# The start of a fused dynamic convolution and feed-forward kernel: first softmax part in two pieces, mask built first, first weights in two loads, row picks between the first units

## The chip, the cores and the metric

The kernel runs on one core of one Trainium2 chip. The time is device microseconds of one execution. The core has a matrix engine (TensorE, PE in the profile; PEld is its weight load), VectorE (DVE), ScalarE (ACT), GpSimd (POOL) and SyncE (SP, which only issues transfers here). They run side by side and wait for one another through semaphores.

## The reference, cut to what matters

Each token has, for each of 8 heads, 7 weights. They go through a softmax and weigh the token's own row of x and the six before it, head by head. The result feeds a feed-forward layer with a squared relu.

```python
w = weight_gen - np.max(weight_gen, axis=-1, keepdims=True)      # (8, 4096, 8, 7)
w = np.exp(w); w = w / (np.sum(w, axis=-1, keepdims=True) + 1e-09)
x_unf = x_pad[:, idx, :].reshape(B, S, K, H, group)              # K = 7, H = 8, group = 24
y = np.einsum('bshk,bskhg->bshg', w, x_unf).reshape(B * S, 192)
h = np.maximum(y @ w_in, 0.0)                                    # w_in: 192 x 2048
out = h * h @ w_out                                              # w_out: 2048 x 192
```

## The kernel before

Tokens are worked in blocks: blocks 0 and 1 of 512 tokens, all later ones of 1024. A block's work is: softmax weights (ScalarE exp, VectorE sum, reciprocal and scale into a tile `v`), rows of `v` brought into the order of the tokens (`wr`), products of `wr` with a band mask that give a banded matrix (`bd`), a convolution as matmuls of x with `bd` into PSUM (`yp`), a cast to fp16 (`y`), and then feed-forward units. A unit is 4 matmuls with w_in in blocks 0 and 1 (6 later) into a PSUM tile `h`, a relu on ScalarE (`t`), and for two units together a squaring on VectorE (`g`). The second matrix product with w_out (`o`) follows in pieces.

For the first two blocks there is no time to send the rows through memory. A "row pick" takes them out of `v` with matmuls against a 0/1 matrix `sel`, eight for one tile of 128 tokens, and ScalarE copies the result out of PSUM. Block 0 and block 1 need five picks each, all from the first softmax part `s0` (8 rows a partition, and 6 rows of the part that follows).

```python
def scale(self, lo, hi, eng):                     # v = ex * rcp, four instructions per 8 rows
    while lo < hi:
        n = min(SL - lo % SL, hi - lo)
        for g in range(HP):
            eng.tensor_tensor(out=..., in0=self.ex[:, lo : lo + n, g],
                in1=self.rcp[:, lo : lo + n, g].unsqueeze(2).broadcast_to((P, n, KK, 2)), op=AluOp.mult)
        lo += n
# [...]
def select_rows(j, s, tiles, places):             # one row pick per tile of 128 tokens
    for i, (pool, tag) in zip(tiles, places):
        pr = pool.tile([P, H * SL], f32, name="pr", tag=tag)
        for r in range(s.r):                      # s.r = 8; HALO = 6
            nc.tensor.matmul(out=pr, lhsT=sel[:, c : c + P], rhs=s.v[:, HALO + r]..., start=(r == 0), stop=(r == s.r - 1))

def copy_rows(j, tiles):                          # PSUM -> wr on ScalarE
    nc.scalar.copy(out=wr_t[j][:, i]..., in_=pr_t.pop((j, i)))

def st_band(j, tiles):                            # bd = wr * mask on VectorE
    nc.vector.tensor_tensor(out=bd_t[j]..., in0=wr_t[j]..., in1=mask..., op=AluOp.mult)
# [...]
spin(21)                                          # 21 warm-up matmuls of 512 columns
row_select(); band_mask()                         # sel, then mask, on GpSimd
s0.load(nc.sync); x_load_f32(0)
load_w_in(w_st, 0, nc.sync)                       # first half of w_in, fp32
load_w_in(w_i[:, 1, 0], 1, nc.gpsimd)             # second half, cast in the transfer
x_load(1); s1.load(nc.gpsimd)
s0.exp(0, s0.rh); s0.total(0, s0.rh); s0.recip(0, s0.rh); s0.scale(0, s0.rh, nc.vector)
# [... row picks, copies and bands of block 0, x casts ...]
st_conv_first(0, next_rows)                       # convolution of block 0; after its first two
                                                  # tiles a row pick of block 1 each, after the
                                                  # second the cast of w_st (ScalarE and VectorE)
select_rows(1, s0, ROW_ORDER[2:4], (o1, o0)); copy_rows(1, ROW_ORDER[2:4])
# [... w_out loads ...]
plans = {
    0: "u P B1 u u u E1 C S1 u u M u u",          # u unit, P row pick, B bands, E exp, C convolution,
    1: "L3 u u B2 M E2 B3 u M E2 u u S2 S2 u M u C u M",   # S rest of softmax, M piece of the second product
    2: "L4 u u u E3 M u u u M B4 u u u u M B5 S3 u u u u M u C E3 u",
    3: "L5 L6 u u u M S3 u u u M u M E4 u u B6 u M u M B7 u u u E4 M u M C S4 u",
}
```

The plan strings give the order in which the steps are written; each engine works through its own instructions in that order.

Of the kernel before, what the change touches and what calls it, by code (L numbers as in the profile page):

```python
# [9 lines left out]
def kernel(  # L10
# [26 lines left out]
    nc = tc.nc  # L37
    f32 = mybir.dt.float32
    f16 = mybir.dt.float16

    B, S, D = x.shape
# [9 lines left out]
    P = 128  # L51
# [16 lines left out]
    BASE = -24  # L68
    starts = [BASE + STEP * i for i in range(NT)]
    bounds = [0, 104, 208, 312, 416, TB]  # L70
    ROW_ORDER = (0, 1, 2, 3, 4)

    AluOp = mybir.AluOpType
    AxisX = mybir.AxisListType.X
# [20 lines left out]
    w_i = const.tile([P, WQ, 2, NQ + NQ // 2], f16, name="w_i")  # L95
    w_p = const.tile([P, WQ, 2, NQ + NQ // 2], f16, name="w_p")
    w_o = const.tile([P, NF, Dm], f16, name="w_o")
    mask = const.tile([P, P, 2], f16, name="mask")
    FIRST = 8
    NSEL = TB + TB - P + FIRST - 1 + P  # L100
# [13 lines left out]

    def band_mask():

        nc.gpsimd.memset(mask, 1.0)
        for sign, base in ((1, 0), (-1, KK - 1)):
            nc.gpsimd.affine_select(
                out=mask, in_=mask, pattern=[[sign, P], [0, 2]], compare_op=AluOp.is_ge,  # L120
                fill=0.0, base=base, channel_multiplier=-sign,
            )

    x_st = {}

    def load_w_in(dst, q, eng):  # L130
        c = q * NQ
        eng.dma_start(out=dst[:, 0:NQ], in_=moe_w_in[0:P, c : c + NQ])
        for r0 in (0, RT):
            eng.dma_start(
                out=dst[r0 : r0 + RT, NQ:], in_=moe_w_in[P:D, c : c + NQ // 2]
            )
            c += NQ // 2

    def cross_w_in(q):
        for r0, r1 in ((0, RT), (RT, 0)):  # L140
# [182 lines left out]
    def x_load(j):  # L323
        x_t[j] = p_x.tile([P, NT, D], f16, name="xt")
        block_load(j, x_t[j], x[j // NBB], D, nc.gpsimd)
# [7 lines left out]
    def x_cast(j, copy, lo, hi):  # L333
        if j not in x_t:
            x_t[j] = p_x.tile([P, NT, D], f16, name="xt")
        copy(
            out=x_t[j][:, lo:hi].rearrange("p t d -> p (t d)"),
            in_=x_st[j][:, lo * D : hi * D],
        )
# [23 lines left out]
    def select_rows(j, s, tiles, places):  # L363

        if j not in wr_t:
            wr_t[j] = p_wr.tile([P, NT, HP, SL * 2], f16, name="wr")
        for i, (pool, tag) in zip(tiles, places):
            pr = pool.tile([P, H * SL], f32, name="pr", tag=tag)
            a = max(j % NBB * TB + tile_start(j, i), 0) - s.t0
            for r in range(s.r):  # L370
                c = a + FIRST - 1 - r
                nc.tensor.matmul(  # L372
                    out=pr, lhsT=sel[:, c : c + P],
                    rhs=s.v[:, HALO + r].rearrange("p g c e -> p (g c e)"),
                    start=(r == 0), stop=(r == s.r - 1),
                )
            pr_t[(j, i)] = pr
# [54 lines left out]
                        for q in (2 * k, 2 * k + 1):  # L432
                            yield later, s, i, q, half, a, b, base

    def st_conv_first(j, between=None):

        s = BLOCKS[j][0]
        y = p_y.tile([P, NK, TB], f16, name="y")
        y_t[j] = y
        if j == 0:  # L440
            yps = [ps_h.tile([P, TB], f32, name="yp", tag="h") for _ in range(2)]
        else:
            yp = ps_h.tile([P, 2, TB], f32, name="yp", tag="h")
            yps = [yp[:, k] for k in (0, 1)]
        places = [(q, 32 * q, 0) for q in range(4)]
        places += [(q, r0 + 32 * (q - 4), 1) for r0 in (0, RT) for q in (4, 5)]
        for i in ROW_ORDER:
            lo, b = bounds[i], bounds[i + 1]
            hi = lo + (STEP if tile_start(s, i) == starts[i] else b - lo)
            bd = bd_t[s][:, H * lo : H * hi].rearrange("p (g c e) -> p g e c", g=HP, e=2)  # L450
            for later in (True, False):
                for q, p0, k in places:
                    _, ha, hb, pre = quads[q]
                    m, h = (32, hb) if later else (pre, ha)
                    nc.tensor.matmul(  # L455
                        out=yps[k][p0 : p0 + m, lo:b],
                        lhsT=x_t[s][:, i, 32 * q : 32 * q + m],
                        rhs=bd[:, h // 2, h % 2, 0 : b - lo],
                        start=True,
                        stop=True,  # L460
                        skip_group_check=True,
                        tile_position=(0, p0),
                    )
            if between:
                between(i)
        if j == 0:
            nc.scalar.copy(out=y[:, 0], in_=yps[0])
            nc.vector.tensor_copy(out=y[:, 1], in_=yps[1])
        else:
            nc.scalar.copy(out=y[:, 0:2], in_=yp)  # L470
# [186 lines left out]
    with nc.allow_low_precision("fp16 matmul pipeline"), tc.manual_schedule():  # L657
# [22 lines left out]
        for v in v_first:  # L680
            nc.vector.memset(v, 0.0)

        wp = ps_o.tile([P, TB], f32, name="wp", tag="o0")

        def spin(n):
            for i in range(n):
                nc.tensor.matmul(out=wp, lhsT=warm[:, 0:P], rhs=warm, start=True, stop=True)

        s0, s1, s2 = parts[:3]
        spin(21)  # L690
        row_select()
        band_mask()
        s0.load(nc.sync)
        w_st = p_wg.tile([P, (R + HALO) * HK], f32, name="w_st", tag="wg")[:, 0 : NQ + NQ // 2]
        x_load_f32(0)
        load_w_in(w_st, 0, nc.sync)
        load_w_in(w_i[:, 1, 0], 1, nc.gpsimd)
        x_load(1)
        s1.load(nc.gpsimd)
        s0.exp(0, s0.rh)  # L700
        s0.total(0, s0.rh)
        s0.recip(0, s0.rh)
        s0.scale(0, s0.rh, nc.vector)
        x_cast(0, nc.scalar.copy, 0, 1)
        x_cast(0, nc.scalar.copy, 1, 3)
        o0, o1, ring = (ps_o, "o0"), (ps_o, "o1"), (ps_h, "h")
        select_rows(0, s0, ROW_ORDER, (o1, ring, ring, ring, o0))
        copy_rows(0, ROW_ORDER[:2])
        x_cast(0, nc.scalar.copy, 3, NT)
        copy_rows(0, ROW_ORDER[2:])  # L710
        for i in ROW_ORDER:
            st_band(0, (i,))

        def next_rows(i):
            n = ROW_ORDER.index(i)
            if n < 2:
                select_rows(1, s0, (i,), ((o1, ring)[n],))
                copy_rows(1, (i,))
            if n == 1:
                c = (NQ + NQ // 2) // 2  # L720
                nc.scalar.copy(out=w_i[:, 0, 0, 0:c], in_=w_st[:, 0:c])
                nc.vector.tensor_copy(out=w_i[:, 0, 0, c:], in_=w_st[:, c:])

        st_conv_first(0, next_rows)
        select_rows(1, s0, ROW_ORDER[2:4], (o1, o0))
        copy_rows(1, ROW_ORDER[2:4])

        nc.gpsimd.tensor_copy(out=gate, in_=w_st[:, 0:1])
        for q in range(4):
            load_w_out(q, 4)  # L730
        s2.load(nc.gpsimd)
        x_load(2)
        nc.gpsimd.memset(v_big, 0.0)

        steady = "MuMuuu" * 3 + "MuuuMCu"
        steady_spread = "MuMuuu" * 2 + "MuCMuuu" + "MuMuuu"
        plans = {  # L740
# [4 lines left out]
        }  # L745


# [110 lines left out]
        for j in range(NBLK):  # L858
            if j + 2 < NBLK:
                load_rows(j + 2)  # L860
            if j == 1:
                for q in range(WQ):
                    cross_w_in(q)
            u = 0
            for step in plans[j].split():
                kind, n = step[0], int(step[1:] or 0)
                if kind == "u":
                    st_unit(j, u)
                    u += 1
                elif kind == "M":  # L870
                    next(mm2)
                elif kind == "C" and j + 1 < NBLK:
                    st_conv(j + 1)
                    if j == 0:
                        x_load(3)
                    elif j + 2 < NBLK:
                        for k in range(BLOCKS[j + 2][0], sum(BLOCKS[j + 2])):
                            x_load(k)
                    if j == 5:
                        load_w_spread()  # L880
                    elif j == 6:
                        cross_w_spread()
                elif kind == "E":
                    parts[n].exp(*next(parts[n].exps))
                elif kind == "S":
                    soft(parts[n])
                elif kind == "B":
                    st_bands(n)
                elif kind == "P":
                    select_rows(1, s0, ROW_ORDER[4:], (o1,))  # L890
                    copy_rows(1, ROW_ORDER[4:])
                elif kind == "L":
                    parts[n].load(nc.sync)

# [46 lines left out]
```

The softmax here doesn't subtract the row's maximum and nothing guards it: scores larger than these inputs give would overflow.

## Time and profile before

| | before |
|---|---|
| time, median of 3 (lowest to highest) | 731.81 us (731.55 to 732.17) |
| span of the profiled execution | 730.0 us |
| PE / DVE / ACT / POOL busy | 724.1 / 626.8 / 612.2 / 99.8 us |
| first unit of block 0 starts | 12.71 us |
| second convolution starts | 16.33 us |
| granted PE clock | 1.00 in all stretches asked for |

The busy times are sums over the whole span. The chain of work that ended last is followed back from the last instruction, step by step, to what released it. In a row of the timeline the bracket at the end gives how long the engine stood idle before it and for whom. The lines themselves stand with the prediction.

### The profile page before, as it was taken

What the parts mean: (1) busy time and instruction counts of PE and PEld (TensorE: products, weight loads), DVE (VectorE), ACT (ScalarE), POOL (GpSimd) and SP (SyncE); (2) the same over time, 40 slices, a digit from 0 to 9 for tenths busy, and PEclk for the clock granted to TensorE, in tenths of its full rate; (3) what the DMA queues carried; (4) which work ended last, traced back from release to release, by engine and by line L of the source; (5) the groups of instructions that cost most, each with busy time, mean ns of one, the idle gap of its engine ahead of it and who ended that gap; (6) DMA issues with size and microseconds to landing.
All of it is one profiled execution on the core that took longest, in us unless ns stands there. A gap on an engine that the chain in (4) does not pass through costs nothing.

```text
span 730.0 us, 30988 instructions
## 1 busy us (share of the span) xinstructions
PE 724.1 (99%) x14053; PEld 528.0 (72%) x14053; DVE 626.8 (86%) x836; ACT 612.2 (84%) x733; POOL 99.8 (14%) x145
## 2 busy tenths in 40 slices
PE   8999999999999999999999999999999999999998
PEld 4657788777777777777777777777777777777777
DVE  7998998998898988888988888988889988778753
ACT  5999888888888888888888888888888888888883
POOL 8131223321001100011001010010000110001000
PEclk9999999999999999999999999999999999999999
DMA  9555455685345452455432554343544325444012
GB/s 202 118 105 115 82 96 105 132 149 129 86 66 138 90 92 59 82 117 124 76 64 61 136 104 88 56 77 116 107 84 86 57 52 119 66 87 78 30 45 68
DMA packets 125984, 68.30 MB, mean 94 GB/s; under 512 B 85321, under 2 KB 122140, under 8 KB 125340
## 3 DMA queue, kind: packets, MB, share of 16 engines
q0 software_dynamic: 46192, 19.43, 22.9%
q1 hardware_dynamic: 79516, 46.79, 22.4%
q8 instruction: 110, 1.80, 1.1%
q14 instruction: 22, 0.18, 0.1%
q10 hardware_dynamic: 144, 0.10, 0.0%
HBM read 50.18 MB, written 28.70 MB: 108 GB/s over the span
## 4 chain that ended last, share of the span: by engine, by line
PE 98%; ACT 1%; DVE 0%; DMA 0%; issue 0%
PE o L621 47%; PE h L572 44%; PE yp L493 4%; PE h L557 2%; PE yp L527 1%; DMA wg<-in_weight_gen_dram 0%; PE yp L455 0%; ACT y L538 0%; DVE v_first L260 0%; PE pr L372 0%; ACT t L586 0%; DVE ssum L245 0%; ACT ex L238 0%; DVE rcp L252 0%; ACT wr L381 0%
## 5 line engine op out<-in xcount | busy, mean ns | idle before, releaser
L586 ACT ACTIVATE t<-h 128x1024 f16<-128x1024 f32 x512 | 496.4, 1026 | 60.3 <-PE h L572 58.8
L621 PEld LDWEIGHTS <-g 64*128 64x128 f16 (+1 forms) x8032 | 344.3, 94 | 55.0 <-issue 2.2
L621 PE MATMUL o<-w_o,g 64*128 64x192 f16 (+1 forms) x8032 | 380.1, 243 | 0.1
L590 DVE TENSOR_TENSOR g<-t 128x2048 f16<-128x2048 f16 (+1 forms) x287 | 307.4, 1105 | 30.1 <-ACT t L586 29.9
L572 PE MATMUL h<-y,w_p 64*128 64x512 f16 x2400 | 291.7, 376 | 0.0
L572 PEld LDWEIGHTS <-w_p 64*128 64x128 f16 x2400 | 113.9, 94 | 94.7
L395 DVE TENSOR_TENSOR bd<-wr,mask 128x4160 f16<-128x4160 f16 (+4 forms) x90 | 149.6, 1686 | 1.3 <-ACT wr L381 0.7
L637 DVE TENSOR_TENSOR o_sb<-o,o_sb 128x384 f32<-128x384 f32 x123 | 68.4, 556 | 61.1 <-ACT o_sb L635 60.1
L321 POOL DMA_DIRECT2D xt<-in_x_dram x63 | 52.6, 839 | 415.3 <-PE yp L493 362.5
L635 ACT COPY o_sb<-o 128x384 f32<-128x384 f32 x129 | 61.6, 477 | 45.9 <-PE o L621 45.1
L572 PE MATMUL h<-y,w_i 64*128 64x512 f16 x576 | 70.6, 376 | 0.3 <-ACT t L586 0.3
L572 PEld LDWEIGHTS <-w_i 64*128 64x128 f16 x576 | 30.3, 94 | 22.2 <-issue 1.6
L493 PEld LDWEIGHTS <-xt 128*32 128x32 f16 x2000 | 24.6, 95 | 10.6 <-issue 10.6
L260 DVE TENSOR_TENSOR v_big<-ex,rcp 128x112 f16<-128x112 f32 (+5 forms) x180 | 29.9, 237 | 1.7 <-DMA vd<-v_big 0.7
L503 DVE CAST y<-yp 128x1024 f16<-128x1024 f32 x25 | 30.4, 1218 | 0.0
L493 PE MATMUL yp<-bd,xt 128*32 128x104 f16 (+1 forms) x2000 | 28.4, 210 | 0.0
L238 ACT ACTIVATE ex<-wg 128x560 f32<-128x560 f32 (+4 forms) x38 | 25.9, 682 | 1.9 <-DMA wg<-in_weight_gen_dram 1.9
L245 DVE TENSOR_REDUCE ssum<-ex 128x80 f32<-128x560 f32 (+4 forms) x38 | 25.3, 666 | 1.3 <-ACT ex L238 1.3
L503 ACT CAST y<-yp 128x1024 f16<-128x1024 f32 x25 | 25.2, 1007 | 0.0
L252 DVE RECIPROCAL rcp<-ssum 128x80 f32<-128x80 f32 (+4 forms) x38 | 22.8, 600 | 1.3
L311 POOL DMA_DIRECT2D xt<-in_x_dram x7 | 3.9, 554 | 120.9 <-PE yp L493 109.4
L355 POOL DMA_DIRECT2D wr<-v_first x24 | 12.9, 560 | 25.1 <-DVE v_first L260 13.6
(41 smaller groups left out, 115.1 us busy)
## 6 DMA issues: line engine op xcount, KB each, us to landing
out_dram<-o_sb SPq DMA_DIRECT2D x63, 384.0 KB
xt<-in_x_dram POOLq DMA_DIRECT2D x42, 240.0 KB, 4.7
wg<-in_weight_gen_dram SPq DMA_DIRECT2D x4, 1064.0 KB
xt<-in_x_dram POOLq DMA_DIRECT2D x21, 192.0 KB, 5.2
wr<-vd SPq DMA_DIRECT2D x38, 80.0 KB
vd<-v_big SPq DMA_DIRECT2D x5, 512.0 KB
y<-y SPq DMA_DIRECT2D x100, 24.0 KB
wg<-in_weight_gen_dram SPq DMA_DIRECT2D x3, 616.0 KB
```

Of the source, the lines that this page charges most:

```text
L238: nc.scalar.activation(out=self.ex[:, lo:hi].rearrange("p r g k e -> p (r g) k e"), in_=self.wg[:, lo:hi].rearrange("p r (g e) k -> p (r g ...
L260: eng.tensor_tensor(out=bass.AP(tensor=v.tensor, offset=v.offset + lo * H * SL + lo % SL * 2 + g * SL * 2, ap=[list(v.ap[0]), [H * SL + 2, ...
L321: eng.dma_start(out=dst[:, first:last], in_=ap)
L395: nc.vector.tensor_tensor(out=bd_t[j][:, H * lo : H * (lo + len(tiles) * n)].rearrange("p (g m c) -> p g m c", g=shape[1], c=2 * SL), in0= ...
L493: nc.tensor.matmul(out=yp[p0 : p0 + 32, k - k0, a:b], lhsT=x_t[s][:, i, c0 : c0 + 32], rhs=bd[:, head // 2, e, 0 : b - a], start=True, sto ...
L503: copy(out=y[:, k0 : k0 + 2], in_=yp)
L572: nc.tensor.matmul(out=h[:, half], lhsT=w_in_chunk(w, u, slot, half), rhs=y_t[j][r0 : r0 + RT, k], start=(slot == 0), stop=(slot == NK - 1 ...
L586: nc.scalar.activation(out=t1[:, e], in_=h, func=ActF.Relu)
L590: nc.vector.tensor_tensor(out=g[:, a : e + 1], in0=t1[:, a : e + 1], in1=t1[:, a : e + 1], op=AluOp.mult)
L621: nc.tensor.matmul(out=oo[:, cc * Dm : (cc + 1) * Dm], lhsT=g[r0 : r0 + n, cc * P : (cc + 1) * P], rhs=w_o[r0 : r0 + n, fc, :], start=(fc ...
L635: nc.scalar.copy(out=o_sb, in_=o[0][:, c])
L637: nc.vector.tensor_tensor(out=o_sb, in0=o[1][:, c], in1=o_sb, op=AluOp.add)
```

## The change

It reshapes the first 20 us and a little of the blocks after.

- The first softmax part is worked as eight rows ("near") and six rows ("far"): two exps and two sums, one reciprocal; VectorE scales the near rows and GpSimd the far rows, so that both work at a time.
- The mask is built ahead of `sel`, at half width (`one`), and doubled by a VectorE copy.
- The first half of w_in comes in two loads of a half each. ScalarE casts the first of them before the `y` copy, VectorE the second after its own `y` copy. The second softmax part's weights now come through SyncE's queue.
- The x casts stand ahead of the row copies on ScalarE.
- Block 1's row picks are taken out of block 0's convolution. One stands behind it, two after unit 0, two after unit 1. Block 1's bands then follow unit 1, and one unit moves ahead of the second convolution.
- The warm-up is 46 matmuls of 234 columns in place of 21 of 512.
- The second exp of the part E3 moves from behind the third convolution into block 3.

```diff
[... the constant ROW_ORDER, (0, 1, 2, 3, 4), goes ...]
@@ -95,6 +94,7 @@
     w_i = const.tile([P, WQ, 2, NQ + NQ // 2], f16, name="w_i")
     w_p = const.tile([P, WQ, 2, NQ + NQ // 2], f16, name="w_p")
     w_o = const.tile([P, NF, Dm], f16, name="w_o")
+    one = const.tile([P, P], f16, name="one")
     mask = const.tile([P, P, 2], f16, name="mask")
     FIRST = 8
     NSEL = TB + TB - P + FIRST - 1 + P
@@ -114,16 +114,13 @@
     def band_mask():
-        nc.gpsimd.memset(mask, 1.0)
+        nc.gpsimd.memset(one, 1.0)
         for sign, base in ((1, 0), (-1, KK - 1)):
             nc.gpsimd.affine_select(
-                out=mask, in_=mask, pattern=[[sign, P], [0, 2]], compare_op=AluOp.is_ge,
+                out=one, in_=one, pattern=[[sign, P]], compare_op=AluOp.is_ge,
                 fill=0.0, base=base, channel_multiplier=-sign,
             )
+        nc.vector.tensor_copy(out=mask, in_=one.unsqueeze(2).broadcast_to((P, P, 2)))
     x_st = {}
@@ -135,6 +132,24 @@
                 out=dst[r0 : r0 + RT, NQ:], in_=moe_w_in[P:D, c : c + NQ // 2]
             )
             c += NQ // 2
+    WH = NQ // 4
+    def load_w_st(dst, n, eng):
+        c = slice(n * WH, (n + 1) * WH)
+        eng.dma_start(
+            out=dst[:, 0:2, c],
+            in_=moe_w_in[0:P, 0:NQ].rearrange("p (a c) -> p a c", a=2)[:, :, c],
+        )
+        for h, r0 in enumerate((0, RT)):
+            c0 = h * NQ // 2 + n * WH
+            eng.dma_start(out=dst[r0 : r0 + RT, 2, c], in_=moe_w_in[P:D, c0 : c0 + WH])
+    def cast_w_st(src, n, copy):
+        c = slice(n * WH, (n + 1) * WH)
+        copy(
+            out=w_i[:, 0, 0].rearrange("p (a c) -> p a c", a=3)[:, :, c], in_=src[:, :, c]
+        )
     def cross_w_in(q):
         for r0, r1 in ((0, RT), (RT, 0)):
[... the convolution of block 0 loses its calls of next_rows ...]
@@ -680,68 +693,69 @@
         for v in v_first:
             nc.vector.memset(v, 0.0)
+        WARM = 234
         wp = ps_o.tile([P, TB], f32, name="wp", tag="o0")
         def spin(n):
             for i in range(n):
-                nc.tensor.matmul(out=wp, lhsT=warm[:, 0:P], rhs=warm, start=True, stop=True)
+                nc.tensor.matmul(
+                    out=wp[:, 0:WARM], lhsT=warm[:, 0:P], rhs=warm[:, 0:WARM],
+                    start=True, stop=True,
+                )
         s0, s1, s2 = parts[:3]
-        spin(21)
+        spin(46)
+        band_mask()
         row_select()
-        band_mask()
         s0.load(nc.sync)
-        w_st = p_wg.tile([P, (R + HALO) * HK], f32, name="w_st", tag="wg")[:, 0 : NQ + NQ // 2]
+        w_st = p_wg.tile([P, (R + HALO) * HK], f32, name="w_st", tag="wg")
+        w_st = w_st[:, 0 : NQ + NQ // 2].rearrange("p (a c) -> p a c", a=3)
         x_load_f32(0)
-        load_w_in(w_st, 0, nc.sync)
+        for n in (0, 1):
+            load_w_st(w_st, n, nc.sync)
+        s1.load(nc.sync)
+        near, far = (0, FIRST), (FIRST, s0.rh)
+        for lo, hi in (near, far):
+            s0.exp(lo, hi)
+            s0.total(lo, hi)
+        s0.recip(0, s0.rh)
+        s0.scale(*far, nc.gpsimd)
+        s0.scale(*near, nc.vector)
+        for lo, hi in ((0, 1), (1, 3), (3, NT)):
+            x_cast(0, nc.scalar.copy, lo, hi)
         load_w_in(w_i[:, 1, 0], 1, nc.gpsimd)
+        o0, o1, ring = (ps_o, "o0"), (ps_o, "o1"), (ps_h, "h")
+        select_rows(0, s0, range(NT), (o1, ring, ring, ring, o0))
+        copy_rows(0, range(NT))
+        for i in range(NT):
+            st_band(0, (i,))
+        cast_w_st(w_st, 0, nc.scalar.copy)
         x_load(1)
-        s1.load(nc.gpsimd)
-        s0.exp(0, s0.rh)
-        s0.total(0, s0.rh)
-        s0.recip(0, s0.rh)
-        s0.scale(0, s0.rh, nc.vector)
-        x_cast(0, nc.scalar.copy, 0, 1)
-        x_cast(0, nc.scalar.copy, 1, 3)
-        o0, o1, ring = (ps_o, "o0"), (ps_o, "o1"), (ps_h, "h")
-        select_rows(0, s0, ROW_ORDER, (o1, ring, ring, ring, o0))
-        copy_rows(0, ROW_ORDER[:2])
-        x_cast(0, nc.scalar.copy, 3, NT)
-        copy_rows(0, ROW_ORDER[2:])
-        for i in ROW_ORDER:
-            st_band(0, (i,))
-        def next_rows(i):
-            n = ROW_ORDER.index(i)
-            if n < 2:
-                select_rows(1, s0, (i,), ((o1, ring)[n],))
-                copy_rows(1, (i,))
-            if n == 1:
-                c = (NQ + NQ // 2) // 2
-                nc.scalar.copy(out=w_i[:, 0, 0, 0:c], in_=w_st[:, 0:c])
-                nc.vector.tensor_copy(out=w_i[:, 0, 0, c:], in_=w_st[:, c:])
-        st_conv_first(0, next_rows)
-        select_rows(1, s0, ROW_ORDER[2:4], (o1, o0))
-        copy_rows(1, ROW_ORDER[2:4])
-        nc.gpsimd.tensor_copy(out=gate, in_=w_st[:, 0:1])
+        picks = iter(zip(range(NT), (o1, o0, o1, o0, o1)))
+        def pick():
+            i, place = next(picks)
+            select_rows(1, s0, (i,), (place,))
+            copy_rows(1, (i,))
+        st_conv_first(0)
+        cast_w_st(w_st, 1, nc.vector.tensor_copy)
+        pick()
+        nc.gpsimd.tensor_copy(out=gate, in_=w_st[:, 0, WH : WH + 1])
         for q in range(4):
             load_w_out(q, 4)
         s2.load(nc.gpsimd)
         x_load(2)
         nc.gpsimd.memset(v_big, 0.0)
         steady = "MuMuuu" * 3 + "MuuuMCu"
         steady_spread = "MuMuuu" * 2 + "MuCMuuu" + "MuMuuu"
         plans = {
-            0: "u P B1 u u u E1 C S1 u u M u u",
+            0: "u P P u P P B1 u u E1 u C S1 u M u u",
             1: "L3 u u B2 M E2 B3 u M E2 u u S2 S2 u M u C u M",
-            2: "L4 u u u E3 M u u u M B4 u u u u M B5 S3 u u u u M u C E3 u",
-            3: "L5 L6 u u u M S3 u u u M u M E4 u u B6 u M u M B7 u u u E4 M u M C S4 u",
+            2: "L4 u u u E3 M u u u M B4 u u u u M B5 S3 u u u u M u C u",
+            3: "L5 L6 u u E3 u M S3 u u u M u M E4 u u B6 u M u M B7 u u u E4 M u M C S4 u",
         }
@@ -887,8 +901,7 @@
                 elif kind == "B":
                     st_bands(n)
                 elif kind == "P":
-                    select_rows(1, s0, ROW_ORDER[4:], (o1,))
-                    copy_rows(1, ROW_ORDER[4:])
+                    pick()
                 elif kind == "L":
                     parts[n].load(nc.sync)
```

More of the change, by code (lines that the diff above doesn't have):

```diff
@@ L70 @@
     bounds = [0, 104, 208, 312, 416, TB]
-    ROW_ORDER = (0, 1, 2, 3, 4)
     AluOp = mybir.AluOpType
@@ L433, in conv_pieces, with st_conv_first @@
                             yield later, s, i, q, half, a, b, base
-    def st_conv_first(j, between=None):
+    def st_conv_first(j):
         s = BLOCKS[j][0]
@@ L463, in st_conv_first @@
                     )
-            if between:
-                between(i)
         if j == 0:
@@ L708 @@
-        copy_rows(0, ROW_ORDER[:2])
-        x_cast(0, nc.scalar.copy, 3, NT)
-        copy_rows(0, ROW_ORDER[2:])
-        for i in ROW_ORDER:
-            st_band(0, (i,))
-        def next_rows(i):
-            n = ROW_ORDER.index(i)
-            if n < 2:
-                select_rows(1, s0, (i,), ((o1, ring)[n],))
-                copy_rows(1, (i,))
-            if n == 1:
-                c = (NQ + NQ // 2) // 2
-                nc.scalar.copy(out=w_i[:, 0, 0, 0:c], in_=w_st[:, 0:c])
-                nc.vector.tensor_copy(out=w_i[:, 0, 0, c:], in_=w_st[:, c:])
@@ new lines @@
+        for lo, hi in ((0, 1), (1, 3), (3, NT)):
+            x_cast(0, nc.scalar.copy, lo, hi)
+        load_w_in(w_i[:, 1, 0], 1, nc.gpsimd)
+        o0, o1, ring = (ps_o, "o0"), (ps_o, "o1"), (ps_h, "h")
+        select_rows(0, s0, range(NT), (o1, ring, ring, ring, o0))
+        copy_rows(0, range(NT))
+        for i in range(NT):
+            st_band(0, (i,))
+        cast_w_st(w_st, 0, nc.scalar.copy)
+        x_load(1)
+        picks = iter(zip(range(NT), (o1, o0, o1, o0, o1)))
[3 more added lines that the diff above has]
+            copy_rows(1, (i,))
```

## The prediction

> **What bounds the kernel now.** I read the page first, then the chain of work that ended last, then the timeline of the first 24 us, then the list of what PE waited for. The page says that TensorE (PE) is busy for 724.1 of 730.0 us, and its summary of the chain that PE holds 98% of it:
>
> ```profile
> PE 724.1 (99%) x14053; PEld 528.0 (72%) x14053; DVE 626.8 (86%) x836; ACT 612.2 (84%) x733; POOL 99.8 (14%) x145
> ```
>
> So the time is three things added: the start of the first feed-forward unit, the PE work after it, and the gaps in that work. The chain over the first 19 us (start us, us, what):
>
> ```profile
> 0.82 3.15 DMA wg<-in_weight_gen_dram
> 3.98 0.94 ACT ex L238
> 4.95 0.98 DVE ssum L245
> 5.96 0.86 DVE rcp L252
> 6.84 1.47 DVE v_first L260 x8
> 8.36 0.35 PE pr L372 x6
> ...
> 12.71 0.91 PE h L557 x4
> 13.62 0.34 PE pr L372 x8
> 13.96 2.37 PE h L557 x12
> 16.33 1.05 PE yp L455 x75
> 17.38 1.61 PE h L557 x8
> ```
>
> Until 12.71 us latencies are strung together. From there every piece begins where the last one ended, all on PE; what is added to PE after 12.71 us is added to the time. The timeline of DVE (start us, us, engine, line, operation):
>
> ```profile
> 9.05 2.60 DVE L395 TENSOR_TENSOR bd<-wr,mask 128x832 f16<-128x832 f16 x5 [0.74 <-ACT wr L381]
> ...
> 12.92 2.46 DVE L395 TENSOR_TENSOR bd<-wr,mask 128x3328 f16<-128x3328 f16 x2
> 15.91 1.23 DVE L590 TENSOR_TENSOR g<-t 128x2048 f16<-128x2048 f16 x1 [0.53 <-ACT t L586]
> ```
>
> The five band products run without a gap, so bands, not row picks, pace the first convolution. The second block's bands are done at 15.38 us, ahead of the first squaring g and of PE's second convolution at 16.33 us. The last view, PE's waits over the whole run (us, times, longest):
>
> ```profile
> PE pr L372 <- DVE v_first L260: 0.8, 2, 0.4
> PE h L572 <- ACT t L586: 0.3, 1, 0.3
> ```
>
> The 0.3 us is at 54.67 us, the only gap charged to another engine between the first unit and the last blocks.
>
> **What the Trainium skill says.** "GPSIMD Engine Reference", section 3.1 Elementwise, puts a two-input elementwise operation on GpSimd at about 2.6 cycles per element at 1.2 GHz plus dispatch, twice VectorE. The kernel before has no such operation to compare with. "SBUF — State Buffer", section Who interferes with whom, says that a DVE instruction with two SBUF inputs contends with a GpSimd instruction that reads SBUF, and that the second one blocks fully. Both halves of the new scaling are such instructions and become ready together; no run here shows it yet. "TensorE: Matmul & The Clock Gate", section What's actually happening, says that PE falls to half clock after about 3.4 us of idling. The trace agrees on the ramp: warm-up matmuls are 0.43 us apart until about 4.2 us and 0.21 us after, having begun at 1.27 us.
>
> **The change, part by part.**
>
> *Softmax in two pieces.* Exp of 448 and 336 elements takes 0.62 to 0.67 and 0.52 us in later blocks of the same trace, the sums 0.61 and 0.50 us, the reciprocal of 112 columns 0.85 us. Exp near ends at about 3.98 + 0.65 = 4.63 us; its sum at 5.26; the far sum at 5.76; the reciprocal at 6.64 us, against 6.82 before. That gains 0.18 us. DVE then scales eight rows in 4 instructions, 0.83 us in the later blocks: done at 7.5 us. GpSimd scales six rows in 4 instructions of 84 elements. My estimate for one: 84 x 2.6 / 1.2 = 182 ns from the GPSIMD page, and some 170 ns of fixed cost, since the trace's one-element GpSimd copy (gate) took 364 ns; so 0.35 us, 1.4 us for four. Beside DVE they would end at 8.1 us, after DVE's (if the port is exclusive) at 8.9 us. I take 8.8, where the kernel before has 8.31: **+0.5 us**. The new program's order shows that all picks but the first two matmuls wait for GpSimd, since picks read rows 6 to 13 and six of those eight are GpSimd's.
>
> *From there to the first unit.* Before: 12.71 - 8.31 = 4.40 us, made of pick, copy, five bands at 0.52 us, last convolution piece, y copy. The picks taken out of the convolution lay in PE's gaps under the bands, and ScalarE's w_in cast (11.29 to 12.12 us) ended together with the convolution (12.07 us). Removing them frees engines that were not the pace: **0**. First unit at about 13.2 us; call this S.
>
> *Mask first, half-width; w_in in two loads; warm-up in 46 matmuls of 234 columns.* The mask ended at 6.27 us before and the first band began at 9.05 us; the gate copy at 9.82 us shows w_in landed 1.5 us before its cast. The warm-up has the same columns (46 x 234 = 10764, 21 x 512 = 10752). **0** for all three. The second weight quarter, issued by GpSimd from 6.23 us before, now follows the scaling and is issued up to 10.7 us, landing 5.1 us later at 15.8; unit 4 wants it at S + 4.6 = 17.8 us. Hidden, with 2 us in hand.
>
> *Row picks between the first units.* Eight pick matmuls cost PE 0.34 us. Before, one pick (8) stood after the first unit and four were hidden. Now one is hidden under the y copy and four (32) follow the first unit: three more on the path, **+1.0 us**.
>
> *The second block's bands.* They now need picks made after unit 1, and in DVE's order they stand behind the first g. Counted from S: unit 0 to 0.9, two picks to 1.6, unit 1 to 2.4; ScalarE's relu of unit 0 to 2.0, two copies of 0.21 to 2.4, relu of unit 1 (1.03 us) to 3.5; DVE's g (1.22) to 4.75; the 3328 band (1.89) to 6.65. PE: two picks to 3.1, units 2, 3 and 4 at 0.77 to 5.4. The convolution needs that band, so PE waits from S + 5.4 to S + 6.65: **+1.3 us**. Before, the bands preceded g and there was no wait. Another 0.1 us goes for PE switching more often between picks and units.
>
> *Exp piece E3 moved* from behind the third block's convolution into the fourth block: takes 0.52 us of ScalarE out from between the y copy and the relu for which PE waited 0.28 us: **-0.3 us**.
>
> Sum: 0.5 + 0 + 1.0 + 1.3 + 0.1 - 0.3 = +2.6 us on 731.81: **734.4 us**. Nothing later gives it back, because PE has no gap left there that a delay could fill.
>
> **Rivals.**
> 1. *GpSimd is quick and truly parallel.* If four instructions take 0.2 us each, picks start at 7.5 us and the start gains 0.8 us. For it: the page's per-element rate alone. Against: the fixed cost and the shared port. Time: 733.1 us.
> 2. *The conv wait is not there* because relus and bands run a little earlier than I string them. Then only picks and scaling remain, 733.1 us; with rival 1, 731.8 us, no change. To be faster than before, the kernel needs both and more.
> 3. *GpSimd is much slower*: its two selects with an inner dimension of 2 took 1.24 us for 256 elements where 1031 in one row took 1.04, so short inner runs may cost it dearly, and the scaling's inner run is 2. Then 0.7 us each, 9.5 us and more: 735.2 us. The weight quarter and x behind it on GpSimd's queue then also come near to being waited for.
> 4. *The clock falls* in the idle stretch between warm-up (7.35 us) and picks. 1.5 us of idling against a stated 3.4, and the convolution behind it loads PE only in part. If it fell, convolution pieces and first units would run at half speed: +2 to +3 us.
>
> **Range and chances.** The terms' uncertainties are -0.8 to +0.8 for the scaling, -1.3 to +0.5 for the conv wait, small for the picks. Together 732.3 to 736.2 us holds it 8 times in 10. A change of 2% is 14.6 us; everything touched lies in the first 55 us of a span that PE fills. Faster by 2%: 0.005; within: 0.985; slower: 0.01.
>
> **What would show it.** Picks' third matmul at 8.8 us, released by GpSimd; start-to-start of the four GpSimd multiplies 0.35 us, and whether DVE's or GpSimd's wait for the other; first unit at 13.2 us; 32 pick matmuls between units 0 and 2; a PE gap of about 1.3 us ahead of the second convolution, released by DVE's bands; no gap near 54 us; from the second block on the same order of pieces as before, 2.6 us later. I am wrong if the first unit starts before 12.5 us, or the second convolution without a wait.

## The result and the profile after

The changed kernel takes 734.43 us (median of 6 runs, 733.64 to 734.96) against 731.96 us (6 runs) for the kernel before: a ratio of 1.0035, 95% interval 1.0022 to 1.0047. A later set of 15 runs of the changed kernel gave 734.03 us against 731.87 us: 1.0025 (1.0018 to 1.0033). It is 2.2 to 2.5 us slower. The one profiled execution of each kernel shows 1.9 us of it: spans of 731.9 and 730.0 us. The profiled execution of the changed kernel took 733.64 us and was the fastest of its six; that of the kernel before took 731.82 us, close to its median. The document comes back to that difference.

The page of the changed kernel, engine busy times. TensorE (PE) has 0.8 us more work by this count and its weight loads (PEld) 4.2 us more, ScalarE 0.6 us more, VectorE 0.3 and GpSimd 1.0 us less:

```profile
PE 724.9 (99%) x14078; PEld 532.2 (73%) x14078; DVE 626.5 (86%) x834; ACT 612.8 (84%) x734; POOL 98.8 (13%) x148
```

The chain of the changed kernel that ended last, its first 20 us (start us, us, what):

```profile
1.26 7.14 PE wp L701 x46
8.40 0.25 PE pr L387 x8
...
8.92 2.61 DVE bd L410 x5
...
12.57 0.92 PE h L570 x4
13.48 0.57 PE pr L387 x16
14.06 0.87 PE h L570 x4
14.93 0.02 issue
14.96 1.03 ACT t L599
15.99 0.02 issue
16.01 1.23 DVE g L603
17.24 1.81 DVE bd L410
19.05 0.14 issue
19.18 1.12 PE yp L470 x72
```

Two things stand against the chain of before. At its head is the warm-up (wp), where the softmax was: in this run the warm-up ended after the scaling, and let the picks (pr) go. And between 14.96 and 19.18 us the chain leaves PE for a relu (t), the squaring (g) and block 1's bands (bd), where before it stayed on PE. PE's waits name it (us, times, longest):

```profile
PE yp L470 <- DVE bd L410: 1.5, 1, 1.5
PE wp L701 <- DVE warm L691: 1.3, 1, 1.3
PE h L570 <- ACT y L480: 0.3, 1, 0.3
```

The first and the third line are new. The third is the first unit's wait for its `y` cast, ahead of 12.57 us, where the kernel before filled PE with row picks. The 0.3 us at 54.67 us, which before had the relu as its releaser, is gone. Lined up piece by piece, the two chains give this account (us):

| stretch | before | after | difference |
|---|---|---|---|
| start of the first unit | 12.71 | 12.57 | -0.14 |
| from there to the second convolution, without the wait, unit 4 counted in both | 4.43 | 5.07 | +0.64 |
| PE's wait ahead of the second convolution | 0 | 1.54 | +1.54 |
| start of the third block's units (34.96 and 37.12): what the rows above leave over | | | +0.12 |
| from there to the end of the first product behind 55 us (56.81 and 58.57) | 21.85 | 21.45 | -0.40 |
| the rest of the span | 673.2 | 673.3 | +0.1 |

(4.43 is 3.62 us from 12.71 to 16.33 and 0.81 us for a unit from the pair at 17.38; 5.07 is 19.18 - 12.57 - 1.54.)

### The profile page after: what moved, and what is told of

Read it like the earlier page. It is cut to its first block, busy times and chain, and to the rows that moved or that the text cites. A ratio compares the mean times of both kernels' runs of the same rounds, so it can differ in the third digit from the quotient of the medians.

```text
span 731.9 us, 31049 instructions
## 1 busy us (share of the span) xinstructions
PE 724.9 (99%) x14078; PEld 532.2 (73%) x14078; DVE 626.5 (86%) x834; ACT 612.8 (84%) x734; POOL 98.8 (13%) x148
## 4 chain that ended last, share of the span: by engine, by line
PE 98%; DVE 1%; ACT 0%; issue 0%
PE o L634 47%; PE h L585 44%; PE yp L506 4%; PE h L570 1%; PE yp L540 1%; PE wp L701 1%; DVE bd L410 1%; PE yp L470 0%; DVE g L603 0%; ACT t L599 0%; PE pr L387 0%; ACT y L480 0%; ACT o_sb L648 0%; DVE warm L691 0%; ACT wr L396 0%
## 5 line engine op out<-in xcount | busy, mean ns | idle before, releaser
L253 ACT ACTIVATE ex<-wg 128x448 f32<-128x448 f32 (+4 forms) x39 | 26.0, 668 | 1.9 <-DMA wg<-in_weight_gen_dram 1.9
L260 DVE TENSOR_REDUCE ssum<-ex 128x64 f32<-128x448 f32 (+4 forms) x39 | 25.3, 652 | 0.9 <-ACT ex L253 0.9
```

The source lines that it names most:

```text
L253: nc.scalar.activation(out=self.ex[:, lo:hi].rearrange("p r g k e -> p (r g) k e"), in_=self.wg[:, lo:hi].rearrange("p r (g e) k -> p (r g ...
```

## The experiments

Each ran beside the kernel before; its medians were 731.98, 732.11 and 731.87 us in the three sets that follow. Times below are medians.

### The picks and the order of block 1's bands: taken out, and alone

The changed kernel with the old place of the picks and the old plan:

```diff
[... st_conv_first calls its new argument after each tile; the second pick's PSUM place is `ring`, as before ...]
-        st_conv_first(0)
+        st_conv_first(0, lambda i: pick() if i < 2 else None)
         cast_w_st(w_st, 1, nc.vector.tensor_copy)
         pick()
+        pick()
[...]
-            0: "u P P u P P B1 u u E1 u C S1 u M u u",
+            0: "u P B1 u u u E1 C S1 u u M u u",
```

> The changed kernel with block 1's row picks, its plan string and its bands where the kernel before has them; softmax in two pieces, mask, loads, warm-up and the moved exp stay as changed. Theory of the prediction: the three extra picks on PE's path (1.0 us) and the wait ahead of the second convolution (1.5 us in the trace of the changed kernel) go, first unit stays at 12.6 us; 734.4 - 2.5 = 731.9 us, about 0.0 against the kernel before. Rival (the loss sits in the start: warm-up, shared port, later weight loads): stays above 733.5 us.

Measured: 731.73 us, ratio 1.0000 (0.9992 to 1.0008). The chain (start us, us, what):

```profile
12.82 0.92 PE h L572 x4
13.74 0.34 PE pr L387 x8
14.08 2.37 PE h L572 x12
16.45 1.06 PE yp L470 x67
```

The pieces follow each other on PE as before the change, although the first unit started later here than in either kernel: the second convolution starts 3.63 us behind the first unit, before the change 3.62. The other way round, the kernel before with only the picks and the plan changed:

```diff
[... next_rows loses its picks and only casts w_in; pick() and the order of places as in the changed kernel ...]
         st_conv_first(0, next_rows)
-        select_rows(1, s0, ROW_ORDER[2:4], (o1, o0))
-        copy_rows(1, ROW_ORDER[2:4])
+        pick()
[...]
-            0: "u P B1 u u u E1 C S1 u u M u u",
+            0: "u P P u P P B1 u u E1 u C S1 u M u u",
```

> The kernel before with only the change's row picks (one behind the first convolution, two after each of the first two units), its order of units and so its place of the bands. Softmax in one piece on VectorE, mask, loads, casts, warm-up and the exp E3 as before. Theory: the same 0.8 us of picks and the same wait of 1.5 us ahead of the second convolution as in the changed kernel appear; 732.0 + 2.3 = 734.3 us, so the whole loss is in this part. Rival (the loss needs the new start too): below 733.2 us.

Measured: 734.27 us, 1.0033 (1.0021 to 1.0045). PE's waits:

```profile
PE yp L455 <- DVE bd L395: 1.5, 1, 1.5
...
PE h L572 <- ACT t L586: 0.3, 1, 0.3
```

The same 1.5 us wait appears with the old start; the convolution starts 6.61 us behind the first unit (12.62 to 19.23), as in the changed kernel. So the whole loss sits in this part: out of the changed kernel it is gone, into the kernel before it is all there. The second line is the old wait near 55 us, since E3 is in its old place here.

### The wait alone

The changed kernel, with nothing swapped but block 1's bands and the squaring of units 0 and 1 on VectorE:

```diff
     nc.scalar.activation(out=t1[:, e], in_=h, func=ActF.Relu)
+    if (j, u) == (0, 1):
+        pick(); pick(); st_bands(1)
     # ... then g of units 0 and 1
-            0: "u P P u P P B1 u u E1 u C S1 u M u u",
+            0: "u P P u u u E1 u C S1 u M u u",
```

> The changed kernel with one thing swapped: on VectorE the bands of block 1 stand before the squaring of units 0 and 1, not after it. PE and ScalarE keep their order, so the picks stay on the path. Theory: the second convolution waits 0.4 us instead of 1.5, a later wait for the squaring may take back up to 0.3; 733.3 to 733.6 us, 0.8 to 1.1 below the changed kernel. Rival (the wait is only a symptom and PE is held elsewhere): no change, 734.4 us.

Measured: 733.04 us (21 runs), 1.0016 (1.0009 to 1.0022); 1.0 us under the 15-run median of the changed kernel, 1.4 under its first, and a little below the 733.3 to 733.6 expected. PE's waits:

```profile
PE wp L710 <- DVE warm L700: 1.3, 1, 1.3
PE yp L470 <- ACT t L604: 0.5, 1, 0.5
```

The wait falls from 1.54 to 0.5 us, and its releaser is now a relu. The order on VectorE was the cause of the larger part. What is left over the kernel before is about 1.1 us. By the trace, where it is 1.3, that is 0.64 us of picks and this 0.5, a first unit 0.24 us later and 0.3 us up to the third block's units, less the 0.4 us of E3 below. Even so ordered, the convolution is held. In the trace the bands start only at 16.49 us, when ScalarE has the last row copies of the late picks out (16.25 to 16.58 us, behind the relu of unit 1). The wide band ends at 18.39 us and the relu that let the convolution go at 18.50. That reading is the trace's; no run tests it.

### The exp E3

Put back in the changed kernel, and moved in the kernel before:

```diff
-            2: "... M u C u",              3: "L5 L6 u u E3 u M S3 u ...",
+            2: "... M u C E3 u",           3: "L5 L6 u u u M S3 u ...",
```

> The changed kernel with the second exp of the third softmax part back behind the third convolution. Theory: PE's wait near 55 us returns and the time grows by 0.3 to 0.4 us, to 734.8 us. Rival (ScalarE has room there): 734.4 us.

> The kernel before with only that exp moved as in the change. Theory: 0.3 to 0.4 us faster than before, 731.6 us, and no wait of PE near 55 us. Rival: 731.96 us, unchanged.

Measured: 734.18 us (6 runs) for the first, 731.71 us (0.9998, 0.9989 to 1.0006) for the second. Neither differs from its partner by more than the runs vary, so the clocked times settle nothing. The traces are plain on the wait: all three profiles with E3 in the old place have 0.3 us of PE waiting for a relu near 55 us, none of the eleven with the new place has it. From the start of the third block's units to the end of the first product behind 55 us the three take 21.84 to 21.85 us, the eleven 21.44 to 21.47. The chain with E3 put back:

```profile
53.97 1.50 ACT y L551 x2
...
55.48 0.30 issue
55.77 1.03 ACT t L599
...
56.85 0.82 PE h L585 x6
57.67 1.32 PE o L634 x32
58.99 1.94 PE h L585 x18
```

The last line starts at 58.99 us here and at 58.57 in the changed kernel, with the first unit at 12.58 and 12.57 us: 0.4 us for the exp, by the trace.

### The split on GpSimd

The changed kernel with all rows on VectorE, and with all rows on GpSimd:

```diff
-        s0.scale(*far, nc.gpsimd)
+        s0.scale(*far, nc.vector)       # first experiment
-        s0.scale(*near, nc.vector)
+        s0.scale(*near, nc.gpsimd)      # second experiment
```

> The changed kernel with all fourteen rows scaled on VectorE, as before the change; the two exps, two sums and everything else stay. Theory that the split on GpSimd brings nothing, because VectorE's and GpSimd's multiplies hold each other up: VectorE's eight take 1.47 us from 6.6 us and end at 8.1 us, where GpSimd's ended too (8.08 us); time as the changed kernel, 734.4 us. Rival (the split helps): 0.3 us or more slower.

> The changed kernel with all fourteen rows scaled on GpSimd, so that no VectorE multiply runs beside it. Measures the disputed cost by itself. If the two engines hold each other up on both sides, GpSimd's multiplies of 84 elements come under 0.28 us apart here, against 0.33 us beside VectorE's; if only VectorE is held up, they stay at 0.33 us. Those of 112 elements about 0.4 us; picks start at about 9.7 us and the time grows by 1.5 us to 735.9 us.

Measured: 734.96 us (4 runs, 1.0039, 1.0026 to 1.0053) and 735.26 us (4 runs, 1.0042, 1.0029 to 1.0056). The timelines, of the changed kernel first (start us, us, engine, line, operation; the idle time before in brackets):

```profile
6.62 1.26 DVE L275 TENSOR_TENSOR v_first<-ex,rcp 128x112 f16<-128x112 f32 x4
6.74 1.34 POOL L275 TENSOR_TENSOR v_first<-ex,rcp 128x84 f16<-128x84 f32 x4 [3.33 <-DVE rcp L267]
```

then with all on VectorE:

```profile
6.69 1.46 DVE L275 TENSOR_TENSOR v_first<-ex,rcp 128x84 f16<-128x84 f32 x8
```

and with all on GpSimd:

```profile
6.91 2.61 POOL L275 TENSOR_TENSOR v_first<-ex,rcp 128x84 f16<-128x84 f32 x8 [3.50 <-ACT xt L351]
```

The scaling lasts 1.46 us with the split (6.62 to 8.08) and 1.46 us without. By the start times in the traces, VectorE's multiplies of 112 elements follow each other after 0.186 us alone and 0.33 us beside GpSimd; GpSimd's of 84 elements after 0.296 us alone and 0.33 us beside VectorE. Side by side, each engine gets one through per 0.33 us. Neither branch of the expectation held for GpSimd: it is held up, but by a tenth; VectorE pays most. (GpSimd's multiplies of 112 elements took 0.35 us where 0.4 was expected, and the time stayed 0.6 us under the 735.9 expected.) The section Who interferes with whom of the Trainium skill's "SBUF — State Buffer" calls the port pair that the two engines share an exclusive lock; that the other instruction "fully blocks" it says of VectorE's two-port modes, and of a VectorE instruction with two SBUF inputs that it contends with GpSimd's reads. Had the multiplies taken turns over their whole length, a pair would have needed 0.186 + 0.296 = 0.48 us; it took 0.33, so they do overlap in part. Split or not, the scaling lasts equally long, and nothing was won by it.

The median with all rows on VectorE lies 0.5 to 0.9 us above the changed kernel's, so the rival's number came true, but its interval overlaps with the changed kernel's and the four runs are 734.20 to 735.99 us. Its trace has one oddity, a cast of w_in on VectorE that took 3.32 us where the changed kernel's took 0.91:

```profile
12.56 3.32 DVE L150 CAST w_i<-w_st 128x768 f16<-128x768 f32 x1
```

GpSimd was issuing the w_out loads at the time in both kernels (11.50 to 14.48 us in the changed one, 10.96 to 13.94 us here), so that alone doesn't explain it. PE's waits with all rows on VectorE:

```profile
PE yp L470 <- DVE bd L410: 0.8, 1, 0.8
PE h L570 <- DVE w_i L150: 0.6, 1, 0.6
PE o L634 <- DVE o_sb L650: 0.6, 1, 0.6
```

The wait for the cast cost nothing. What PE lost there it no longer lost ahead of the second convolution (0.8 us in place of 1.5), which starts 6.61 us behind the first unit here (12.53 to 19.14) as in the changed kernel. The span is 0.7 us longer because of the third line, at 133 us: VectorE had come late to its sum into `o_sb` after waiting 2.0 us for a transfer (`vd`), for which the changed kernel's VectorE waited 1.4 us. Why the transfer was later, and whether that happens more often without the split, isn't shown.

### The cast and the warm-up

The cast on ScalarE, where ScalarE stood idle, and ten warm-up matmuls fewer:

```diff
         cast_w_st(w_st, 0, nc.scalar.copy)
+        cast_w_st(w_st, 1, nc.scalar.copy)        # first experiment
-        cast_w_st(w_st, 1, nc.vector.tensor_copy)
-        spin(46)
+        spin(36)                                  # second experiment
```

> The changed kernel with the second half of the first w_in cast on ScalarE right after the first half, ahead of its y copy, instead of on VectorE behind its y copy. There VectorE's cast ran beside GpSimd's issue of the w_out loads and took 0.68 to 0.92 us, once 3.32 us, against 0.55 us in the kernel before. Theory that this collision adds a varying delay to units 2 and later: median 0.2 to 0.6 us below the changed kernel's, about 734.0 us, and runs closer together. Rival (the cast is hidden): 734.4 us, unchanged.

> The changed kernel with 36 warm-up matmuls in place of 46. Theory: the warm-up's end, not the scaling, lets the first picks go (8.2 to 8.8 us in the traces so far, later when the clock rises later), so with ten fewer the picks start at 8.1 us with GpSimd's last multiply, the median falls by 0.2 to 0.5 us to about 734.1 us and the runs lie closer together. Rival (the scaling sets the start): 734.4 us, or slower if the picks then meet a slow clock.

Measured: 733.79 us (7 runs), 1.0027 (1.0016 to 1.0038), and 733.72 us (12 runs), 1.0027 (1.0019 to 1.0036). The changed kernel, run again for comparison:

> The changed kernel as it is, beside the others on one chip, for a larger number of runs and a second profile. Theory: 734.4 us; wait of 1.5 us ahead of the second convolution again; the first picks start when the warm-up ends, at 8.1 to 8.9 us depending on when the clock rises.

gave 1.0025 (1.0018 to 1.0033). So neither edit moves the time by an amount that can be told; both theories fall as far as the median goes, and the runs did not lie closer together with the shorter warm-up (733.1 to 735.26 us). The slowest of those has a mean granted clock of 0.997 where the others have 1.000; a fall of the clock behind the shorter warm-up, which the expectation's rival names, would look so, but that run has no profile.

The mechanism of the warm-up is there, though only in part of the profiles. The matmuls in the traces follow each other twice as fast from the moment at which PE's clock doubles (0.20 and 0.10 us apart for 234 columns), and that moment differs from run to run. (The clock column of the view by stretches reads 1.00 ahead of it too.) Six profiles have the same start up to the picks, with the split and 46 warm-up matmuls (us):

| profile | clock doubles | scaling ends | third pick matmul | first unit |
|---|---|---|---|---|
| cast on ScalarE | 4.2 | 8.19 | 8.24 | 12.51 |
| changed kernel, run again | 4.9 | 7.79 | 7.85 | 12.11 |
| E3 put back | 5.6 | 8.26 | 8.31 | 12.58 |
| changed kernel, first profile | 6.2 | 8.08 | 8.30 | 12.57 |
| picks and plan of before | 6.7 | 8.08 | 8.55 | 12.82 |
| bands first | 6.9 | 8.12 | 8.67 | 12.95 |

In the first three rows the picks' third matmul starts 0.05 us behind GpSimd's last multiply, as the prediction had it; in the last three the warm-up still held PE, and the picks came 0.2 to 0.55 us behind the scaling. So the expectation that the first picks start when the warm-up ends, at 8.1 us or later, failed for the changed kernel run again. Its first unit is 0.84 us ahead of that with the bands first: 0.5 us are the warm-up's, and 0.3 us come from the scaling, which was earlier because the first softmax weights had landed earlier (exp at 3.73 and 4.06 us). With 36 matmuls the picks wait for the scaling again. Start times from 12.1 to 13.0 us cover more than the 0.14 us by which the change seemed to gain in the first pair of profiles, so that gain isn't shown. With the old warm-up the clock doubled at 4.1, 4.3 and 5.1 us in the three profiles there are; whether the new shape of the warm-up makes that moment later isn't shown either.

### What the start can give without the picks

Picks and plan of before with the new start and 36 warm-up matmuls; and the same with the cast on ScalarE:

> The changed kernel with the row picks, the plan string and bands of the kernel before and with 36 warm-up matmuls: everything of the change kept that cost nothing. Theory: picks at 8.1 us, first unit at 12.5 us, no PE wait after it: 731.4 us, 0.5 us below the kernel before. Rival (the start has no more to give): 731.8 to 732.0 us.

> Row picks, plan and bands as in the kernel before, 36 warm-up matmuls, the second w_in cast on ScalarE, the rest as changed. Theory: first unit at 12.4 us, no PE wait behind it; 731.4 us, 0.5 us below the kernel before. Rival (the start has no more to give, or runs vary more than that): 731.7 to 732.0 us.

Measured: 731.76 us (0.9996, 0.9988 to 1.0004) and 731.84 us (1.0000, 0.9992 to 1.0009). The first units start at 12.44 and 12.37 us and no wait of PE follows before the second convolution, as expected; three profiles with the start of before have 12.62 to 12.77 us. The medians don't show that gain. In the two profiles a later wait spends it, 0.72 us at 130.7 us for a sum into `o_sb` and 0.39 us at 141.3 us with no releaser seen; the kernel before had neither in its profile. Whether the earlier start brings such waits about isn't shown. No version was found that beats the kernel before by more than the runs vary.

## Why the prediction came out right

The time was foretold as 734.4 us and measured as 734.43, later 734.03. The cause named as the larger one, the wait ahead of the second convolution, is the cause, and the order of bands and squaring behind it is shown by experiment. But the sum is closer than its terms, and that part is luck. One of the prediction's own signs of being wrong also came up: a first unit before 12.5 us, which the changed kernel run again has at 12.11 us. It says that the start was foretold wrongly, and doesn't touch the wait.

- *The wait of the second convolution, +1.3 us*: 1.54 us, and the string of steps holds: counted from the first unit, the squaring was to end at 4.75 us and did at 4.67, the convolution was to start at 6.65 us and did at 6.61. Right, shown by the kernel before with this part alone. The wait came out longer because PE was done with unit 4 sooner, at 5.07 us and not at 5.4.
- *Three more picks, +1.0 us and 0.1 us for switching*: 0.64 us by the chains, 0.76 with what is left over up to the third block. Mis-sized. The term multiplied the 0.34 us of a lone pick; two in a row take 0.57 us, not 0.68, which makes 1.14 - 0.34 = 0.80 us.
- *The scaling, +0.5 us*: wrong. The step that failed took the shared port to be nearly exclusive. The two engines overlapped in part and the scaling ended at 8.08 us, not 8.8; the prediction's other figure, 8.1 us side by side, was the right one. The estimate of a GpSimd multiply (0.35 us) was near, at 0.296 us alone and 0.33 beside VectorE, though its 170 ns of fixed cost don't follow from a one-element copy of 364 ns; by the multiplies of 84 and 112 elements alone (0.296 and 0.348 us) it is some 1.9 ns per element and 0.14 us. In the first profile the warm-up's end let the picks go, which no step of the prediction had: it counted the same columns, and the clock doubled 2 us later than in the profile before.
- *From the scaling to the first unit, 0; mask, loads, second weight quarter, 0*: the way from the first pick's copy to the first unit was 3.90 us (8.67 to 12.57), before 3.98 (8.73 to 12.71). No wait of PE for the later weight quarter showed in any profile.
- *E3, -0.3 us*: 0.4 us by the traces; not to be told in the clocked medians.
- *The clock falling* (fourth rival): not in the changed kernel. It did fall in the kernel with all rows on GpSimd, in two of its four runs.
- *The range*: its upper end of 736.2 us is 0.5 us more than the uncertainties named add up to (734.4 + 0.8 + 0.5 = 735.7).

By the chains the terms come to -0.14 + 0.76 + 1.54 - 0.40 = 1.76 us, with 0.1 to 0.2 us at the end of the span 1.9. The prediction had 2.6. The medians say 2.2 to 2.5, so between 0.3 and 0.6 us of the measured loss is in no piece of the first profile, and that it brought the total close to 2.6 is the luck. The profiled execution was 0.8 us below the median of its six. The later 15 runs fall into two groups, seven of 733.05 to 733.53 us and eight of 734.03 to 734.53, and the profile taken there (733.20 us) is of the lower one; none shows the upper. The start (clock, landing of the weights) varies between executions, and some profiles of other kernels have a wait of 0.2 to 0.7 us deep in the run. Which of them makes up the remainder stays open; the two experiments aimed at it, the cast and the warm-up, did not find it.

## What to carry to other kernels

Where one engine runs without gaps, work taken from a gap on it ahead of that stretch and put into the stretch costs its length there (0.6 to 0.8 us for three more picks), whatever it frees elsewhere; ask which engine's wait the work was hidden under before moving it. A product that the bound engine needs soon must stand ahead of one that it needs later in the in-order queue of the engine that makes both: swapping the two took back two thirds of the wait. When a trace of one run and the medians differ by up to a quarter of the effect, do not hang small terms on the trace alone. And a wait is a loss only if what follows it comes later: the 0.6 us for the slow cast was taken out of a wait that stood behind it.

## What was not expected of the hardware

In the kernel with all rows on GpSimd PE waited 2.0 us for the scaling, and 1.7 us after the wait had ended its clock fell to half for 3.4 us, in the midst of picks and convolution. The stretches of that profile (us, their length, busy us and count for PE, PEld, DVE, ACT, POOL, then clock and transfers):

```profile
10.00:11.50 1.50, 1.38 (x55) 1.15 (x55) 1.25 (x3) 1.41 (x6) 1.50 (x4) 0.93 0.27 34
11.50:14.00 2.50, 2.46 (x72) 1.76 (x72) 1.89 (x4) 0.98 (x3) 2.50 (x5) 0.50 1.06 156
14.00:15.50 1.50, 1.48 (x15) 0.51 (x15) 0.85 (x2) 0.41 (x2) 1.50 (x3) 0.76 1.39 149
```

PE counts as busy for 2.46 of 2.50 us while its clock is at 0.50. The section What's actually happening of the Trainium skill's "TensorE: Matmul & The Clock Gate" has the clock fall after an idle window of about 3.4 us; here the longest wait was 2.0 us, with thin work behind it. The clock of this trace doubled at 4.47 us, fell at 11.30 and doubled again at 14.71, and these times are two and one times 3.413 us apart; in the other 13 profiles the first doubling and the fall at the kernel's end are 727.04 or 723.63 us apart, 213 or 212 times 3.413. So the clock changes in steps of that length here. The step ahead of the fall (7.89 to 11.30 us) held 1.7 us of the wait and then the picks and the convolution's beginning. By its mean clock the fall came in two of the kernel's four runs (0.998 at 735.53 and 735.56 us; 1.000 at 734.89 and 735.00), which would fit a wait that lies differently to the steps; no run tests that. And two engines' multiplies of the same kind ran at 0.33 us a pair, between the 0.296 us of the slower one alone and the 0.48 us of taking turns.
